# A tail with three more tiles turned on TensorE, and an even plan for the DMAs of the backward attention loop

## The chip, the cores and the metric

The kernel runs on one core of one Trainium2 chip. The metric is device time in microseconds (us) of one execution. Lower is better. The core has a matmul engine (PE in the profile, its weight loads PEld), VectorE (DVE), ScalarE (ACT), GpSimd (POOL) and SyncE (SP), and queues of DMAs that SP, ACT and POOL issue.

## The reference

One transformer block, forward and backward: layer norm with a modulation from a conditioning vector, attention with 32 heads of width 16 over 2048 tokens of width 512, a second modulated norm, and a two-layer net with a squared ReLU. The output of the block and the gradients of nine inputs are wanted.

```python
def _fwd_reference(A_x, A_wqkv, A_wo, B_x, B_w1, B_b1, B_w2, B_b2, c, w_mod):
    ...
    mod = (_silu(c) @ w_mod).reshape(c.shape[0], 6, 1, -1)
    sa, ca, ga, sb, cb, gb = (mod[:, 0].copy(), mod[:, 1].copy(), mod[:, 2].copy(), mod[:, 3].copy(), mod[:, 4].copy(), mod[:, 5].copy())
    h = _layernorm(x, axis=-1) * (1 + ca) + sa
    x = x + ga * _A_ref(h, A_wqkv, A_wo)
    h = _layernorm(x, axis=-1) * (1 + cb) + sb
    x = x + gb * _B_ref(h, B_w1, B_b1, B_w2, B_b2)
    return x
...
    _out, _vjp = jax.vjp(_f, A_x, A_wqkv, A_wo, B_w1, B_b1, B_w2, B_b2, c, w_mod)
    _grads = _vjp(grad_out)
    _out0 = jnp.asarray(_out)
    return (_out0, *[jnp.asarray(_g) for _g in _grads])
```

`_A_ref` is the attention (`x @ wqkv`, softmax of the scaled scores, `@ wo`), `_B_ref` the net. All arrays are bf16.

## The kernel before

The forward pass, the net and its gradients fill the first 1120 us and are not touched. The change lies in the two stages behind them.

**The loop** is the backward pass of the attention. It runs over 8 groups of 4 heads (called heads here, `hg`), and in each over 4 chunks of 512 keys (`kc`) and 16 tiles of 128 queries, so 512 units. For each unit PE makes the scores of four heads (`score`), ACT their exponentials `E_u` (`expo`), PE the products with the gradient `dO` (`dp_pair`, two per unit, each of two heads), DVE multiplies these with `E_u` into `dS_u` (L1600), and PE sums the gradients of keys and values in `accVK` (`k_quad`, `v_quad`) and of queries in `dqacc` (`dq_quad`), the last from a transposed `dS`. Most of `dS` is transposed by DMA from SP (L1615, L1617), one unit of eight on PE (`pe_turn`). Four units make a block.

The order of the work on each engine is written by hand: the strings `order_t` and `order_n` list the steps of a block, and `manual_schedule` keeps each engine to that order. The step `D` counts the pairs of products (`nD`, 128 to a head, 1024 in all). After each `D` all the DMAs that `at(j, ...)` has put down for a pair up to that count are issued. `load` issues them from ACT, in line with its exponentials. They are

- per head 22 loads for the next head (`kvq_loads`, `row_loads`: q, k, v, dO rows and two auxiliary rows), planned by `plan_head`, and the step `spread_qz` on POOL,
- the stores of a head's dV/dK columns, one per `kc` (L1657), and of its dQ, four rows of 16 (L1689), in DRAM tensors `dVKtP` and `dQc`,
- in heads 4 to 6, 24 loads of `wT_st`, the transposed `wqkv`, into columns 0 to 255 of `KS_tok` and `dOs_tok`, which the heads 0 to 3 have left,
- in the last head 40 loads of 16 rows that bring back four groups of dV/dK (`xs["vk", 0]` to `xs["vk", 3]`) and one tile of dQ (`xs["dq", 0]`).

**The tail** begins before the last units are done. Its inputs are eight tiles of dV/dK and four of dQ (`xs`), each 128 rows of features by 2048 tokens. It does two things with them. `dh1(t, srcs)` (L1778) multiplies 128 tokens of each tile with the turned weights, twelve matmuls per token tile `t`, seven of them early (`early7`) and five late (`late`), whose tiles arrive last; `ln_grad`, `norm_tile` and `dx_out` carry the result through the layer norm on DVE and ACT. `dwqkv` (L1970) multiplies the normed input `h1J` with the tiles in token order: 12 blocks of 16 matmuls, four on `tokA` (dV/dK 0 to 3), four on `tokB` (dV/dK 4 to 7), four on `KS_tok` (dQ). For that each tile is transposed: `turn_vk` does it on PE with copies on DVE (tiles 0 to 3, into `tokA`), `turn_dma` by a DMA from SP (tiles 4 to 7 and all four of dQ). dQ goes into `KS_tok`, whose columns 0 to 255 hold turned weights until the last `dh1`.

Beside this the tail makes the gradient of the modulation: `mod_row(k)` (L1872) is one matmul that picks a row out of `rowsb` (a copy by POOL of the sums, two rows of it scaled by DVE in `factors`) into a bank `px`, and an ACT copy to `dmodb`; `row_sums(g)` sums four token tiles each into the banks `accVK` and `px`; `wmod_grad` and `c_grad` use the rows, the latter with `w_mod`, which `load_wmod` brings in from SP once the space of `xs["vk", 0]` to `xs["vk", 3]` is free.

Loop and tail are two `manual_schedule` parts (L1714 and L1994).

Of the kernel before, what the change touches and what calls it, by code (L numbers as in the profile page):

```python
# [34 lines left out]
def kernel(  # L35
# [1499 lines left out]
    with ExitStack() as ph:  # L1535
# [134 lines left out]
        def dq_out(b):  # L1670
# [30 lines left out]
        for hg in range(1, HG):  # L1701
            plan_head(hg)
        pieces = []
        for i, key in enumerate(("q", "k", "v", "do")):
            xs["vk", i] = hsets[0][key][:]
        xs["dq", 0] = qz[0].rearrange("p t h d -> p (t h d)")
        for (key, i), dsrc in zip([("vk", 0), ("vk", 1), ("vk", 2), ("vk", 3), ("dq", 0)], (dVKtP,) * 4 + (dQc,)):
            pieces += [(xs[key, i][r:r + 16, :], dsrc[i][r:r + 16, :]) for r in range(0, P, 16)]
        for i, (to, fro) in enumerate(pieces):
            at((HG - 1) * 128 + 14 + 27 * i // 10, load, to, fro)  # L1710
        for i in range(24):
            j, r = i // 2, slice(64 * (i % 2), 64 * (i % 2) + 64)
            at((4 + i // 8) * 128 + 106 + 4 * (i % 8), load, w_rows(j)[r], wT_st[j].rearrange("p (a b) -> p a b", a=2)[r])
        with tc.manual_schedule(engines={PE.engine, ACT.engine, DVE.engine, SP.engine, POOL.engine}):  # L1714
# [68 lines left out]
            def turn_vk(i):  # L1783
                for g in range(2):
# [4 lines left out]
                    for i8 in range(8):  # L1789
                        t = 8 * g + i8  # L1790
                        PE.transpose(pt[:, i8, :], xs["vk", i][:, t * P:(t + 1) * P], identb[:])
                    DVE.tensor_copy(tokA[:, i, 8 * g:8 * g + 8, :], pt[:])
# [28 lines left out]
            turn_vk(0)  # L1821
# [12 lines left out]
    with ExitStack() as ph:  # L1834
# [3 lines left out]
        rowsb = big.tile([P, D], BF, name="rowsb")  # L1838
# [16 lines left out]
        def constants():  # L1855
            POOL.memset(thirty2[:], 1.0 / 32)
            POOL.tensor_copy(selb[:], identb.rearrange("p (j c) -> p j c", c=32)[:, :, 0:1].to_broadcast([P, 4, P]))
            POOL.tensor_copy(rowsb[0:97, :], sums[0:97, :])
# [4 lines left out]
        def factors():  # L1863
            DVE.tensor_scalar(nrd[:], rstd1[:], -1.0 / D, None, ALU.mult)
            DVE.reciprocal(rec4, cb1_bc)
            for r in (32, 64):
                DVE.tensor_tensor(rowsb[r:r + 1, :], sums[r:r + 1, :], rec4[r:r + 1, :], ALU.mult)

        def mod_row(k):
            j = (5, 3, 4, 2)[k]  # L1870
            pm = psx.tile([P, 512], F32, name="pmod", tag="px")
            PE.matmul(pm[:], selb[0:97, k, :], rowsb[0:97, :], start=True, stop=True)  # L1872
# [90 lines left out]
        def dwqkv(n, b, ic):  # L1963
# [7 lines left out]
            wblk = big.tile([P, D], BF, name="wqblk", tag="wqblk", bufs=3)  # L1971
# [12 lines left out]
        def turn_dma(key, i):  # L1984
            if key == "vk":
                if not tokB:
                    tokB["t"] = tpool.tile([P, 4, TT, P], BF, name="dvk_tokB", tag="dsT")
# [6 lines left out]
        with tc.manual_schedule(engines={PE.engine, ACT.engine, DVE.engine, SP.engine, POOL.engine}):  # L1994
# [11 lines left out]
            for t in range(2):  # L2006
                dh1(t, early7[6:])
            for t in range(2, 6):
                dh1(t, early7)
            load_x0(3)  # L2010
            for t in range(TT):
# [4 lines left out]
                if 1 <= t < 5:  # L2016
                    mod_row(t - 1)
# [6 lines left out]
                if t in (6, 8, 10, 12):  # L2024
# [95 lines left out]
```

## Time and profile before

| | us |
|---|---|
| median of 3 runs | 2492.26 |
| lowest, highest | 2484.49, 2504.86 |
| the profiled execution | 2491.55 |
| its span | 2489.4 |
| the loop, first to last product on DVE (1120.1 to 2372.9) | 1252.8 |
| from there to the end | 116.5 |

Over the span PE is busy 93%, ACT 92%, DVE 73%, POOL 15%. The busy time of PE does not mean that it runs at its peak, since matmuls overlap: a 512-column matmul is recorded with some 380 ns and the next starts some 216 ns after it. So the tail is read by the times at which groups of matmuls begin and end, and by who ended PE's waits. In a table of stretches the columns are the length, the busy time and the number of instructions of each engine, the granted share of the TensorE clock, the share of the DMA engines and the GB/s. The chain of waits is read from its end back: each line is a start, a length, and the work or DMA that the next line waited for.

### The profile page before, as it was taken

The page shows a single profiled execution, that of the slowest core. Times are in us where ns is not written, and L with a number is a line of the kernel's source. Part 1 is how long each engine was busy: PE and PEld are TensorE (multiplying, and loading weights), DVE is VectorE, ACT ScalarE, POOL GpSimd, SP SyncE. Part 2 cuts the span into 40 slices and gives each one's busy share as a digit, 9 for nine tenths or more (in the row PEclk, how much of TensorE's full clock was granted, in tenths as well). Part 3 has the DMA queues.
Part 4 walks back from the last instruction along what each step waited for, and adds up shares of the span by engine and source line. Part 5 has one row for each costly group of instructions (what it writes and reads, how often), then busy time and mean ns, then how long its engine had stood idle before and what let it go on. Part 6 is the DMA issues. An engine that isn't in the chain of part 4 may idle for free.

```text
span 2489.4 us, 49493 instructions
## 1 busy us (share of the span) xinstructions
PE 2313.2 (93%) x18745; PEld 767.8 (31%) x18826; DVE 1809.5 (73%) x2354; ACT 2301.3 (92%) x3582; POOL 372.5 (15%) x412
## 2 busy tenths in 40 slices
PE   8898889989988998999999999999999999999988
PEld 3232223222322332442323223333332223332233
DVE  5555153454435454578999999999999999998974
ACT  7999999999989999639999999999999999999953
POOL 2000000211323142201111101111011110110112
PEclk9999999999999999999999999999999999999999
DMA  4466555366757765979999999999999999999997
GB/s 141 134 170 170 152 123 131 97 163 144 104 85 172 152 120 131 253 228 171 206 201 198 204 202 200 209 206 206 207 207 210 198 207 203 205 205 204 194 221 174
DMA packets 1222523, 442.38 MB, mean 178 GB/s; under 512 B 1099246, under 2 KB 1195116, under 8 KB 1222028
## 3 DMA queue, kind: packets, MB, share of 16 engines
q1 hardware_dynamic: 1186028, 393.47, 82.6%
q0 software_dynamic: 14544, 23.47, 5.9%
q10 hardware_dynamic: 21712, 22.27, 3.7%
q8 instruction: 148, 2.42, 0.4%
q14 instruction: 91, 0.75, 0.1%
HBM read 94.63 MB, written 70.78 MB: 66 GB/s over the span
## 4 chain that ended last, share of the span: by engine, by line
ACT 42%; PE 38%; issue 8%; DVE 6%; DMA 3%; SPq 1%; ACTq 1%; POOL 0%; another core or an unknown queue 0%; DVEq 0%; POOLq 0%
ACT E_u L1584 24%; ACT ET L566 13%; PE dqacc L1667 4%; PE psST L564 4%; PE psS_A L1578 3%; PE pm L232 3%; ACT dsT L1754 2%; PE accVK L1640 2%; PE psS_B L1578 2%; PE oacc L580 2%; PE pm L413 2%; PE pm L399 2%; PE psS_C L1578 2%; PE accVK L1649 2%; PE pm L488 1%
## 5 line engine op out<-in xcount | busy, mean ns | idle before, releaser
L1600 DVE TENSOR_TENSOR dS_u<-psD_u,E_u 128x1024 bf16<-128x1024 f32 x1024 | 1186.9, 1218 | 69.0 <-PE psD_u L1598 27.8
L566 ACT ACTIVATE ET<-psST 128x1024 bf16<-128x1024 f32 x1024 | 941.3, 1257 | 19.5 <-PE psST L564 19.1
L1584 ACT ACTIVATE E_u<-psS_A 128x512 bf16<-128x512 f32 x768 | 508.4, 662 | 12.3 <-PE psS_C L1578 8.5
L1584 ACT ACTIVATE E_u<-psS_B 128x512 bf16<-128x512 f32 x768 | 502.2, 654 | 7.1 <-PE psD_u L1598 2.1
L1598 PE MATMUL psD_u<-iv,ido 32*128 32x512 bf16 x2048 | 408.9, 388 | 0.0
L564 PE MATMUL psST<-qt_sb,kt_sb 32*128 32x512 bf16 x2048 | 317.3, 385 | 61.2 <-ACT ET L566 46.5
L1584 ACT ACTIVATE E_u<-psS_C 128x512 bf16<-128x512 f32 x512 | 333.2, 651 | 4.0 <-PE accVK L1649 1.7
L1578 PE MATMUL psS_A<-ik,iq 32*128 32x512 bf16 x768 | 293.5, 382 | 12.8 <-ACT E_u L1584 2.7
L1578 PE MATMUL psS_B<-ik,iq 32*128 32x512 bf16 x768 | 295.3, 384 | 9.3 <-ACT E_u L1584 1.6
L1578 PEld LDWEIGHTS <-iq 32*128 32x128 bf16 x2048 | 130.1, 91 | 318.1 <-issue 300.7
L1640 PE MATMUL accVK<-dS_u,qz 128*32 128x512 bf16 x2048 | 212.0, 390 | 0.2 <-PE psD_u L1598 0.2
L580 PE MATMUL oacc<-ET,vaug 128*32 128x512 bf16 x2048 | 207.1, 394 | 3.0 <-DVE ostage L584 3.0
L1685 POOL TENSOR_TENSOR dQacc<-dQacc,dqtmp 128x512 f32<-128x512 f32 x64 | 81.2, 1268 | 853.4 <-ACT dqtmp L1680 729.2
L1649 PE MATMUL accVK<-E_u,dOs_tok 128*16 128x512 bf16 x2048 | 203.5, 387 | 0.0
L1578 PE MATMUL psS_C<-ik,iq 32*128 32x512 bf16 x512 | 194.6, 380 | 5.4 <-ACT E_u L1584 1.2
L564 PEld LDWEIGHTS <-kt_sb 32*128 32x128 bf16 x2048 | 85.7, 91 | 349.0 <-issue 324.5
L1667 PE MATMUL dqacc<-dsT,KS_tok 128*32 128x512 bf16 x2048 | 147.3, 386 | 14.3 <-ACT E_u L1584 0.7
L1754 ACT ACTIVATE dsT<-ptT 128x1024 bf16<-128x1024 bf16 x126 | 143.5, 1139 | 5.6 <-PE ptT L1630 5.0
L250 DVE COPY part<-pm 128x512 f32<-128x512 f32 (+2 forms) x103 | 63.5, 617 | 112.4 <-PE pm L232 105.6
L1598 PEld LDWEIGHTS <-ido 32*128 32x128 bf16 x2048 | 104.4, 91 | 96.3 <-issue 90.8
L1640 PEld LDWEIGHTS <-qz 128*32 128x32 bf16 x2048 | 58.1, 94 | 180.5 <-issue 166.0
L584 DVE COPY ostage<-oacc 128x512 f32<-128x512 f32 x32 | 22.1, 689 | 101.0 <-PE oacc L580 87.1
(417 smaller groups left out, 2524.2 us busy)
## 6 DMA issues: line engine op xcount, KB each, us to landing
p_st<-part POOLq DMA_DIRECT2D x36, 256.0 KB, 5.1
kt_sb<-qkT_st SPq DMA_DIRECT2D x124, 64.0 KB
wA<-in_B_w_dram SPq DMA_DIRECT2D x28, 256.0 KB
wB<-w1T_st SPq DMA_DIRECT2D x21, 256.0 KB
wA<-w2T_st SPq DMA_DIRECT2D x21, 256.0 KB
wB<-in_B_w_dram SPq DMA_DIRECT2D x21, 256.0 KB
p_st<-part POOLq DMA_DIRECT2D x25, 192.0 KB, 4.9
p_st<-part SPq DMA_DIRECT2D x18, 256.0 KB
```

The source lines that it names most:

```text
L564: PE.matmul(ps[:, hi, :], kt_sb[r:r + 32, kt * P:(kt + 1) * P], qt_sb[r:r + 32, :], start=True, stop=True, tile_position=(r, 0))
L566: ACT.activation(ET[:, 2 * pair:2 * pair + 2, :], ps[:], AF.Exp, scale=SCALE)
L580: PE.matmul(oacc[32 * hq:32 * hq + 32, :], lhsT, ET[:, hq, :], start=(kt == 0), stop=(kt == TT - 1), tile_position=(0, 32 * hq), skip_grou ...
L1578: PE.matmul(psS[:], st["q"][r:r + 32, qt * P:(qt + 1) * P], st["k"][r:r + 32, kc * 512:kc * 512 + 512], start=True, stop=True, tile_positi ...
L1584: ACT.activation(bst[u][0][:, hq, :], sst.pop((u, hq))[:], AF.Exp, scale=SCALE)
L1598: PE.matmul(psD[:, hi, :], st["do"][r:r + 32, qt * P:(qt + 1) * P], st["v"][r:r + 32, kc * 512:kc * 512 + 512], start=True, stop=True, til ...
L1600: DVE.tensor_tensor(dS_u[:, 2 * pair:2 * pair + 2, :], psD[:], E_u[:, 2 * pair:2 * pair + 2, :], ALU.mult)
L1640: PE.matmul(cur["vk"][32 * hq:32 * hq + 32, :], hst[hg]["qz"][:, qt, hq, :], bst[u][1][:, hq, :], start=(qt == 0), stop=False, tile_positi ...
L1649: PE.matmul(acc[32 * hq:32 * hq + DH, :], dOs_tok[:, qt, (hg * 4 + hq) * DH:(hg * 4 + hq + 1) * DH], E_u[:, hq, :], start=False, stop=(qt ...
L1667: PE.matmul(acc[32 * hq:32 * hq + 32, :], KS_tok[:, kc * 4 + kt, h * DH:h * DH + 32], tT[:, :, hq * 4 + kt, :], start=(kt == 0), stop=(kt ...
L1685: POOL.tensor_tensor(dst2, dst, tmp[:], ALU.add)
L1754: ACT.activation(dst, pt[:], AF.Identity)
```

## The change

The loop's DMAs get one plan per head. `plan_head(h)` now lists all loads of a head (for the last head the 40 pieces; in heads 4 to 6 eight `wT_st` loads each are put between) and the stores that will come up in it, and gives each a place: the k-th of `count` at pair 10 + 111 k / count of the head. A store takes a place once its earliest pair has come; a load takes one from pair 14 on. What is left over goes behind pair 124. The stores keep to their place or to the moment when their data is there, whichever is later. The `wT_st` loads are cut by columns (128 rows of 256) and not by rows (64 rows of 2 x 256).

In the tail, dV/dK tiles 6 and 7 and the dQ tile 3 are turned on PE, the last with ACT copies. The other three dQ transposes alternate with the loads of `w_mod`. Two rows of the modulation (0 and 3) are picked before the loop over token tiles, from a second copy of the sums, the other two at tiles 4 and 5; two x loads go behind the last dQ rows on SP; the row sums come one tile later, the third behind the first block of `dwqkv`. Loop and tail become one schedule. `wqblk` shares the buffers of `xn1b`.

```diff
-        def plan_head(hg):
-            j0 = (hg - 1) * 128 + 14
-            loads = list(kvq_loads(hg)) + list(row_loads(hsets[hg % 2]["do"], dOT_st, hg, slice(0, n), d_st))
-            for i, (to, fro) in enumerate(loads):
-                at(j0 + (4 * i if i < 4 else 36 + 36 * (i - 4) // 10), load, to, fro)
-            at(j0 + 40, spread_qz, hg)
+        store_at = {}
+
+        def plan_head(h):
+            loads = []
+            if h + 1 < HG:
+                loads += list(kvq_loads(h + 1)) + list(row_loads(hsets[(h + 1) % 2]["do"], dOT_st, h + 1, slice(0, n), d_st))
+            else:
...
+            if 4 <= h < 7:
+                for i in range(8 * (h - 4), 8 * (h - 4) + 8):
+                    j, a = divmod(i, 2)
+                    loads.insert(6 + 3 * (i % 8), (w_rows(j)[:, a, :], wT_st[j][:, 256 * a:256 * a + 256]))
+            stores = [(26 + i, ("dq", h - 1, i)) for i in range(4) if h > 0]
+            stores += [(32 * kc + 41, ("vk", h, kc)) for kc in range(3) if h < HG - 2]
+            stores += [(9, ("vk", h - 1, 3)) for _ in range(1) if 0 < h < HG - 1]
+            stores.sort()
+            count = len(loads) + len(stores)
+            for k in range(count):
+                j = 10 + 111 * k // count
+                if stores and (stores[0][0] <= j or not loads):
+                    store_at[stores.pop(0)[1]] = h * 128 + j
+                elif j >= 14:
+                    at(h * 128 + j, load, *loads.pop(0))
+            for k, (to, fro) in enumerate(loads):
+                at(h * 128 + 124 + k, load, to, fro)
...
+            if h + 1 < HG:
+                at(h * 128 + 54, spread_qz, h + 1)
...
-                    at(cur["j"] + 4, load, dVKtP[hg][:, part], hst[hg]["vk"][:, part])
+                    at(max(cur["j"] + 4, store_at["vk", hg, kc]), load, dVKtP[hg][:, part], hst[hg]["vk"][:, part])
...
-                    at(hg * 128 + 158 + 4 * hq, load, dQc[hg // 2, r:r + DH, :], st["dq"][32 * hq:32 * hq + DH, :])
+                    at(max(cur["j"] + 6, store_at["dq", hg, hq]), load, dQc[hg // 2, r:r + DH, :], st["dq"][32 * hq:32 * hq + DH, :])
...
-        for i, (to, fro) in enumerate(pieces):
-            at((HG - 1) * 128 + 14 + 27 * i // 10, load, to, fro)
-        for i in range(24):
-            j, r = i // 2, slice(64 * (i % 2), 64 * (i % 2) + 64)
-            at((4 + i // 8) * 128 + 106 + 4 * (i % 8), load, w_rows(j)[r], wT_st[j].rearrange("p (a b) -> p a b", a=2)[r])
...
+        hold.enter_context(tc.manual_schedule(engines={PE.engine, ACT.engine, DVE.engine, SP.engine, POOL.engine}))
...
-        with tc.manual_schedule(engines={PE.engine, ACT.engine, DVE.engine, SP.engine, POOL.engine}):
-            for g in range(3):
+        if True:
+            for g in range(2):
                 load_x0(g)
             nb1_rows()
-            turn_vk(1)
+            turn_vk(("vk", 1), tokA[:, 1])
             last_dq(B_last, slice(3 * 512, n))
             constants()
-            turn_vk(2)
-            turn_vk(3)
+            load_x0(2)
+            load_x0(3)
+            turn_vk(("vk", 2), tokA[:, 2])
+            turn_vk(("vk", 3), tokA[:, 3])
+            tokB["t"] = tpool.tile([P, 4, TT, P], BF, name="dvk_tokB", tag="dsT")
+            for t in range(2):
+                dh1(t, early7[6:])
+            mod_row(0, "px")
+            turn_vk(("vk", 6), tokB["t"][:, 2])
+            dh1(2, early7)
+            mod_row(3, "accVK")
+            turn_vk(("vk", 7), tokB["t"][:, 3])
             factors()
             norm_tile(0)
             norm_tile(1)
-            for t in range(2):
-                dh1(t, early7[6:])
-            for t in range(2, 6):
+            for t in range(3, 6):
                 dh1(t, early7)
-            load_x0(3)
             for t in range(TT):
...
-                if 1 <= t < 5:
-                    mod_row(t - 1)
+                if 4 <= t < 6:
+                    mod_row(t - 3, ("accVK", "px")[t - 4])
...
-                if t in (6, 8, 10, 12):
+                if t in (6, 8):
                     turn_dma("vk", 1 + t // 2)
...
-                if t % 4 == 3 and t > 4:
-                    row_sums(t // 4 - 1)
+                if t % 4 == 0 and t > 4:
+                    row_sums(t // 4 - 2)
             for i in range(4):
+                if i < 3:
+                    turn_dma("dq", i)
                 load_wmod(i)
-            for i in range(4):
-                turn_dma("dq", i)
...
                 if k == 0:
+                    row_sums(2)
                     dx_out(TT - 1)
...
+                if k == 4:
+                    turn_vk(("dq", 3), KS_tok[:, :, 3 * P:4 * P], ACT)
```

More of the change, by code (lines that the diff above doesn't have):

```diff
@@ L1790, in turn_vk @@
                         t = 8 * g + i8
-                        PE.transpose(pt[:, i8, :], xs["vk", i][:, t * P:(t + 1) * P], identb[:])
-                    DVE.tensor_copy(tokA[:, i, 8 * g:8 * g + 8, :], pt[:])
+                        PE.transpose(pt[:, i8, :], xs[i][:, t * P:(t + 1) * P], identb[:])
+                    if eng is DVE:
+                        DVE.tensor_copy(dst[:, 8 * g:8 * g + 8, :], pt[:])
+                    else:
+                        ACT.activation(dst[:, 8 * g:8 * g + 8, :], pt[:], AF.Identity)
             def copy_turn(half):
@@ L1837 @@
         rec1, rec4 = (hsets[i]["qs"].rearrange("p t e -> p (t e)").bitcast(F32) for i in range(2))
-        rowsb = big.tile([P, D], BF, name="rowsb")
+        rowsb = [big.tile([P, D], BF, name=f"rowsb{i}") for i in range(2)]
         selb = big.tile([P, 4, P], BF, name="selb")
@@ L1857, in constants @@
             POOL.tensor_copy(selb[:], identb.rearrange("p (j c) -> p j c", c=32)[:, :, 0:1].to_broadcast([P, 4, P]))
-            POOL.tensor_copy(rowsb[0:97, :], sums[0:97, :])
+            for i in range(2):
+                POOL.tensor_copy(rowsb[i][0:97, :], sums[0:97, :])
         def nb1_rows():
@@ L1866, in factors, with mod_row @@
             for r in (32, 64):
-                DVE.tensor_tensor(rowsb[r:r + 1, :], sums[r:r + 1, :], rec4[r:r + 1, :], ALU.mult)
-        def mod_row(k):
+                DVE.tensor_tensor(rowsb[1][r:r + 1, :], sums[r:r + 1, :], rec4[r:r + 1, :], ALU.mult)
+        def mod_row(k, tag):
             j = (5, 3, 4, 2)[k]
-            pm = psx.tile([P, 512], F32, name="pmod", tag="px")
-            PE.matmul(pm[:], selb[0:97, k, :], rowsb[0:97, :], start=True, stop=True)
+            pm = psx.tile([P, 512], F32, name="pmod", tag=tag)
+            PE.matmul(pm[:], selb[0:97, k, :], rowsb[int(k % 3 != 0)][0:97, :], start=True, stop=True)
             ACT.activation(dmodb[:, j, :], pm[:], AF.Identity)
@@ L1993 @@
         early7 = early + (("vk", 7),)
-        with tc.manual_schedule(engines={PE.engine, ACT.engine, DVE.engine, SP.engine, POOL.engine}):
-            for g in range(3):
+        if True:
+            for g in range(2):
                 load_x0(g)
             nb1_rows()
-            turn_vk(1)
+            turn_vk(("vk", 1), tokA[:, 1])
             last_dq(B_last, slice(3 * 512, n))
             constants()
-            turn_vk(2)
-            turn_vk(3)
+            load_x0(2)
[10 more added lines that the diff above has]
+            turn_vk(("vk", 7), tokB["t"][:, 3])
             factors()
```

23 lines of the change are left out of this document (11 added, 12 removed).

## The prediction

> **What bounds the kernel now.** I read the page for the span, then the stretches (a table by windows), then the chain of waits through the end, then the waits of each engine. The profiled execution took 2491.55 us by the clock outside, 2489.4 us of it span; 2.15 us lie around it. The median of the runs is 2492.26, so sums against 2491.55 need +0.7.
>
> ```profile
> span 2489.4 us, 49493 instructions
> ```
>
> The stretches, each with its length, then busy time and instructions of PE, PEld, DVE, ACT and POOL, the granted clock, the DMA share and GB/s. First the loop of eight heads (1024 pairs of products on DVE, 128 to a head), then its best head (3) and its last (7), then the tail in six pieces.
>
> ```profile
> core 0: us, PE busy (x) PEld busy (x) DVE busy (x) ACT busy (x) POOL busy (x), PEclk, DMA share, GB/s
> 1120.10:2372.90 1252.80, 1205.43 (x11466) 374.37 (x11466) 1185.64 (x1023) 1224.20 (x2329) 145.53 (x106) 0.98 1.20 202
> 1591.10:1745.30 154.20, 148.72 (x1442) 46.86 (x1440) 148.13 (x129) 153.05 (x293) 17.95 (x13) 1.00 1.20 207
> 2214.20:2372.90 158.70, 151.92 (x1430) 46.12 (x1428) 147.46 (x128) 151.99 (x288) 15.22 (x12) 0.96 1.22 201
> 2372.90:2384.40 11.50, 11.01 (x152) 7.24 (x151) 6.23 (x10) 3.78 (x5) 2.19 (x2) 1.00 1.12 229
> 2384.40:2395.30 10.90, 7.74 (x39) 3.33 (x37) 6.26 (x7) 1.60 (x3) 1.61 (x4) 1.00 0.83 221
> 2395.30:2405.80 10.50, 7.50 (x25) 2.78 (x26) 9.22 (x26) 7.78 (x12) 1.29 (x1) 0.84 0.85 287
> 2405.80:2434.80 29.00, 29.00 (x151) 12.38 (x150) 24.57 (x65) 20.77 (x29) 6.98 (x7) 1.00 1.02 171
> 2434.80:2464.90 30.10, 30.10 (x144) 13.16 (x140) 22.92 (x61) 14.31 (x31) 9.91 (x14) 1.00 1.12 257
> 2464.90:2489.40 24.50, 16.37 (x64) 6.90 (x65) 0.00 (x0) 5.58 (x11) 3.48 (x6) 0.82 0.26 81
> ```
>
> The loop has PE, DVE and ACT all at 95% or more: a head without disturbance costs 154.2 us, eight of them 1233.6, so the loop loses 19.2 us to single stalls. The tail is TensorE's: two pieces are full, and what is lost stands in three, where PE is idle or its clock is below 1. Who ends those waits, on PE in the tail:
>
> ```profile
> PE pwx L1970 <- DMA KS_tok<-iq: 3.9, 1, 3.9
> PE pmod L1872 <- ACT dmodb L1873: 3.0, 3, 1.3
> PE pdh L1778 <- DMA iq<-dQst: 2.3, 1, 2.3
> PE pdh L1778 <- DMA qz<-dVKtP: 0.8, 1, 0.8
> ```
>
> So 10.0 us of waits (total, times, longest), each touched by the change. The chain through the end shows what the clock adds:
>
> ```profile
> 2412.26 0.55 PE rsumJ L1942 x8
> 2412.80 10.47 PE pdh L1778 x48
> ...
> 2434.83 7.01 PE pwq L1970 x32
> ...
> 2468.82 0.59 PE pwx L1970
> 2469.41 0.22 issue
> 2469.63 5.34 PE pwx L1970 x14
> ```
>
> A 512-column matmul costs 10.47/48 = 0.218 us in step, a block of dwqkv (16) 7.01/2 = 3.5 us; the block behind the wait for KS_tok took 0.59 + 0.22 + 5.34 = 6.15, 2.65 too long, at the clock of 0.82.
>
> **The change, part by part.** Signs: minus is time won.
>
> *Three more tiles on PE.* The price of a turned tile, by the nearest rows (the same helper, same shapes), with the work of DVE and POOL that stands around the place where two of them go:
>
> ```profile
> 2383.54 1.06 PE L1791 MATMUL ptv<-identb,ido 128*128 128x128 bf16 x16
> ```
> ```profile
> 2383.90 1.88 DVE L1792 COPY dvk_tokA<-ptv 128x1024 bf16<-128x1024 bf16 x3
> 2385.69 0.35 DVE L1864 TENSOR_SCALAR rstd<-rstd 128x16 f32<-128x16 f32 x1
> 2385.95 3.34 DVE L1865 RECIPROCAL iqs<-modbc 128x512 f32<-128x512 bf16 x1
> 2389.39 1.38 DVE L1867 TENSOR_TENSOR rowsb<-r_inv,iqs 1x512 bf16<-1x512 f32 x2
> ```
> ```profile
> 2385.40 0.61 POOL L1858 CAST rowsb<-r_inv 97x512 bf16<-97x512 f32 x1
> ```
>
> About 1.0 us of PE each. Tiles 6 and 7 fall into 2384.4 to 2395.3, where PE has 10.90 - 7.74 = 3.16 us idle, waiting for dV/dK and dQ rows. Two mod rows come along (0.44 us). Row 0 waits for POOL's copy of the sums, ready at 2385.40 + 0.61 = 2386.0; PE stands there two matmuls after 2384.4, at 2384.9, so a wait of 1.1 us, with all of dh1 queued behind it. Stretch: 7.74 + 2.0 + 0.44 + 1.1 = 11.3 against 10.9, **+0.4**. The rows that PE waited for (2.3 and 0.8 us) are met 0.4 us after they used to land, and SP now issues the dQ rows ahead of two x loads that stood before them, so they should cost nothing. DVE gains four copies (1.88/3 = 0.63 each, 2.5 us) ahead of the 5.1 us of factors; its first dxn comes at about 2396, as before.
>
> *Mod rows out of the first tiles.* In 2395.3 to 2405.8 the pmod matmuls wait 3.0 us for ACT's copies out of the one bank; 25 matmuls at 0.218 need 5.45 us, were busy 7.50, at a clock of 0.84, after the waits before it. If neither is left: -3.0 - 2.05, and two rows (0.44) gone: **-5.5**. Late next is DVE: in the full stretch its six instructions a tile cost 24.57/65 x 6 = 2.27 us, PE's twelve matmuls 2.62, so PE stays the slower. The two rows that stay at tiles 4 and 5 hold both banks that the first row sums need; their wait for ACT costs about one of the three pmod waits, **+1.0** (0 to 1.3). The third row sums only move (0.55 us) behind dwqkv 0.
>
> *dQ: three transposes between the w_mod loads, one on PE.* The rows of SP's issues now:
>
> ```profile
> 2437.40 12.45 SPq L1991 DMA_TRANSPOSE KS_tok<-qz  x1
> 2449.89 5.26 SPq L1991 DMA_TRANSPOSE KS_tok<-ik  x1
> 2455.19 4.80 SPq L1991 DMA_TRANSPOSE KS_tok<-ido  x1
> ```
>
> The first stood behind eight loads. It now comes first, as soon as dh1's last matmul frees the columns of KS_tok that held the turned weights. Row sums stood behind that matmul, so it ended at 2434.83 - 0.55 = 2434.3; with the terms so far, 4.1 less, it is 2430.2. Three transposes take 5 us each; the eight loads cost the first 12.45 - 5 = 7.5, so the four that now lie ahead of the last cost 3.7; 5 us to land (the flight of 4.98 below): 2430.2 + 15 + 3.7 + 5 = 2454. The first block that reads them starts eight blocks later, 2430.2 + 8 x 3.5 = 2458 even without the row sums, totals and turned tile between. So no wait: **-3.9 - 2.65**, and **+1.0** for the tile turned on PE; its two ACT copies lie in a stretch where ACT is busy 14.31 of 30.10 us.
>
> *One schedule.* The order on PE, DVE, ACT and SP within the loop is unchanged but for ACT's DMA issues; DVE's small factor for the mean moves from the program's start to here (about the 0.35 of L1864, DVE idle): 0.
>
> *The even plan in the loop.* Places: one DMA per 3.7 pairs in heads 1 to 3 (30 of them in 111 pairs), 2.9 in heads 4 to 6, 2.5 in head 7. Before, 18 loads lay in 61 pairs (one per 3.4) with stores added, and in head 7 one per 2.7 with four dQ stores thrown among them. There the trace has a stall:
>
> ```profile
> 2251.57 8.46 DMA dsT<-dS_u
> 2260.03 0.02 issue
> 2260.05 0.33 ACTq L1560
> ```
>
> ACT's issue of a load waited until SP's transpose of 8.46 us had landed; the exps queued behind it on ACT, PE ran short and its clock fell (0.96 in that head). Head 7 lost 158.7 - 154.2 = 4.5 us. Spaced, I expect most of this back. The other heads' losses show no DMA that I can name, so I give them nothing: **-3** (-19.2 if all vanish, +6 if a like stall comes up in a head that has none). By the Trainium skill (DMA: Bandwidth & Descriptors, Issuing engines are not separate DMA queues) DMAs of all issuers run on the same 16 engines, so spreading wins no bandwidth; the trace's DMA share of 1.20 to 1.22 in good and bad heads agrees. By it this term would be 0.
>
> *End of the loop.* The plan leaves two of head 7's pieces over, put behind the 124th pair; in ACT's order the last has five exps behind it. Row of the first of those five, of the matmuls that need the piece, and of a load's flight there:
>
> ```profile
> 2369.88 0.60 ACT L1584 ACTIVATE E_u<-psS_B 128x512 bf16<-128x512 f32 x1
> ```
> ```profile
> 2372.66 1.40 PE pdh L1778 x6
> ...
> 2380.66 4.98 DMA iv<-dVKtP
> ```
>
> 2369.9 + 4.98 = 2374.9; the sixth matmul stands at 2373.9: **+1.0** (0, or 4.4 with the flight of 8.46).
>
> Sum: 0.4 - 5.5 + 1.0 - 6.55 + 1.0 - 3 + 1.0 = **-11.7**; 2491.55 - 11.7 = 2479.9, say **2480 us**.
>
> **The rivals.** *The dQ transposes are late all the same* (2488 to 2494): at 12.45 us each, as the one behind eight loads, they land at 2430 + 37 + 5 = 2472, a wait of some 11 us, and the clock falls again (2.65): 2480 + 14 = 2494; at half of that wait 2488. For it: POOL's output DMAs run at the same time. Against: the two later ones took 5.26 and 4.80 beside the same outputs. 0.14.
>
> *A late last row at every head* (2514, slower): the plan leaves one load of each head, the delta row of the next, for pair 124, four pairs (4 x 154.2/128 = 4.8 us) ahead of the matmul that reads it. The flights in the rows are 4.98 to 8.46. If it comes late, seven times a stall like the one in head 7: 7 x 4.5 = 31.5, less the tail's 8.7. It decides once the flight passes the lead. Against: ACT's exps run ahead of DVE's products, which lengthens the lead by a pair or two. 0.08.
>
> *The loop loses its stalls altogether* (2464): -19.2 in place of -3. For: an even load of the DMA queues. Against: the clock dips in heads without any late DMA. 0.12.
>
> *The clock halves under the turned tiles* (2491): 11.3 us of work in that stretch at half clock in the worst case. Against: the stretch 2372.9 to 2384.4, most of its 152 PE instructions transposes, was granted 1.00. 0.05. The Trainium skill (TensorE: Matmul & The Clock Gate, PE-mode transpose) says that transposes do not count as busy for the clock and cost about 275 ns each in a kernel; 48 of them would be 13 us, not 3, an estimate that makes 2490. The trace's 16 in 1.06 us speaks against that.
>
> **How the numbers follow.** The forecast has 0.61. About 1% (25 us) is what this kernel's measurement tells from no change. Own range of the forecast: terms of unknown size (loop -8 to +3, end of loop to +4.4, row sums) and the scatter of the runs: 2469 to 2492. The late transposes lie in it or at 2494; 2464 and 2497 leave out half of the loop's best case, most of the slow one and a little else. Faster than 2467.3 needs the loop's gain: 0.11. Slower than 2517 needs the late row at its worst: 0.04. Within 1%: 0.85.
>
> **What would show it.** In the tail: no PE wait for KS_tok and the blocks of dwqkv even at 3.5; pmod waits of at most 1.3 us together; dh1's last matmul near 2430 (less what the loop wins); one new wait on POOL's sums. In the loop: head 7 near 155, no ACT issue waiting for a transpose. Wrong would be: the chain through a DMA of KS_tok again, PE waiting for ido at each head's first products, or clock dips in more heads than before.

## The result, and the profile after

| | before | after |
|---|---|---|
| median | 2492.26 us (11 runs, 2478.7 to 2504.86) | 2476.98 us (11 runs, 2471.62 to 2486.92) |
| ratio to before, 95% interval | | 0.9946, 0.9923 to 0.9969 |
| profiled execution, span | 2491.55, 2489.4 us | 2478.99, 2477.2 us |
| the loop, first to last product on DVE | 1252.8 us | 1250.3 us |
| from there to the end | 116.5 us | 105.4 us |

The forecast was 2480 us, the range 2464 to 2497. The interval leaves out 1: the kernel is faster by 0.5%, within the 1% of "no change". Of the 12.2 us between the two spans, 11.1 lie in the tail.

The stretches of the changed kernel, with the columns of before: the loop, its last head, then the tail from the last product on.

```profile
span 2477.2 us, 49668 instructions
```
```profile
core 0: us, PE busy (x) PEld busy (x) DVE busy (x) ACT busy (x) POOL busy (x), PEclk, DMA share, GB/s
1121.50:2371.80 1250.30, 1206.98 (x11466) 375.77 (x11466) 1183.82 (x1024) 1224.15 (x2329) 145.85 (x106) 0.98 1.20 203
2217.10:2371.80 154.70, 149.42 (x1428) 46.70 (x1428) 146.85 (x129) 151.29 (x288) 15.23 (x12) 0.99 1.24 204
2371.80:2384.00 12.20, 11.01 (x153) 7.28 (x151) 6.31 (x11) 3.78 (x5) 2.23 (x2) 1.00 1.12 241
2384.00:2396.00 12.00, 10.96 (x77) 5.86 (x75) 9.29 (x13) 3.42 (x5) 2.11 (x5) 1.00 0.84 216
2396.00:2408.50 12.50, 12.50 (x59) 5.55 (x57) 11.94 (x34) 9.18 (x12) 2.50 (x2) 1.00 1.04 265
2408.50:2428.50 20.00, 19.89 (x103) 8.59 (x102) 19.37 (x54) 17.00 (x25) 5.36 (x5) 1.00 0.83 151
2428.50:2450.00 21.50, 21.50 (x119) 9.77 (x118) 11.59 (x21) 11.67 (x24) 7.32 (x10) 1.00 1.08 222
2450.00:2474.00 24.00, 23.91 (x112) 10.67 (x109) 12.28 (x42) 10.05 (x20) 6.51 (x11) 1.00 0.60 191
```

Before, three of the tail's stretches had PE idle by 3 to 8 us, two of them with a clock of 0.82 to 0.84. Now the clock is 1.00 in all, and PE waits more than 0.25 us in two places only. These are the waits of PE over the tail (total, times, longest):

```profile
PE pmod L1893 <- POOL rowsb L1879: 1.0, 1, 1.0
PE dqacc L1694 <- DMA dsT<-dS_u: 1.0, 1, 1.0
```

The second still belongs to the loop (its last dQ products). The chain of waits through the end shows how solid the rest is. Its columns are start, length, work:

```profile
2390.46 3.25 DVE iqs L1886
...
2395.22 0.69 DVE dxn L1936
...
2408.53 0.59 ACT dmodb L1894
...
2409.56 10.47 PE pdh L1795 x48
2420.03 0.55 PE rsumJ L1963 x8
2420.57 7.88 PE pdh L1795 x36
2428.45 3.45 PE pwq L1991 x16
...
2448.73 0.89 PE ptv L1808 x16
...
2459.99 3.45 PE pwx L1991 x16
2463.44 6.91 PE pwq L1991 x32
2470.35 3.47 PE pwx L1991 x16
```

The chain of before ran through a DMA of `KS_tok` and 5.34 us of slow matmuls. Now it passes through DVE's `factors` and norm gradients up to 2408, and from there through matmuls alone. The blocks of `dwqkv` are even at 3.45 to 3.56, and the four that read `KS_tok` begin at 2459.99 without a wait; the last transpose into it had landed at 2456.0.

### The profile page after: what moved, and what is told of

The parts are those of the page before. It is cut to its first block, busy times and chain, and to the rows that moved or that the text cites. A ratio compares the mean times of both kernels' runs of the same rounds, so it can differ in the third digit from the quotient of the medians.

```text
span 2477.2 us, 49668 instructions
## 1 busy us (share of the span) xinstructions
PE 2321.9 (94%) x18874; PEld 770.8 (31%) x18874; DVE 1809.2 (73%) x2358; ACT 2303.7 (93%) x3584; POOL 372.6 (15%) x413
## 5 line engine op out<-in xcount | busy, mean ns | idle before, releaser
L1605 PE MATMUL psS_A<-ik,iq 32*128 32x512 bf16 x768 | 293.2, 382 | 11.2 <-DVE dwlast L236 0.9
```

Source lines behind the costliest of these rows:

```text
L1605: PE.matmul(psS[:], st["q"][r:r + 32, qt * P:(qt + 1) * P], st["k"][r:r + 32, kc * 512:kc * 512 + 512], start=True, stop=True, tile_positi ...
```

## The experiments

All edits are against the changed kernel unless they say otherwise (minus: its line; plus: the experiment's). "Tail" is the time from the last product on DVE to the end, "loop" from the first to the last product, both from the trace. A "spell" is a stretch in which the trace shows TensorE's granted clock at half. Where one run is named, a difference in its whole time of some us tells nothing, and its trace is read instead.

**Each kernel once more.**

> The changed kernel once more, for a second trace. If the halvings of the TensorE clock in the loop are chance (a matter of phase), they fall in other heads than in the first trace (where they cost heads 1, 0 and 5 most) while their number stays 6 to 12 and the tail agrees within 0.5 us; if the DMA plan makes them, they come back in the same heads and at the same pairs. Time 2472 to 2485.

> The kernel before once more, for a second trace of it. Theory A, its tail is a fixed 116 to 117 us with a wait of 3 to 5 us for the last dQ tile: then the tail's gain of 11 us belongs whole to the changed tail. Rival B, that wait comes and goes with what still moves on the DMA engines when dh1 ends, as in the kernel with the old tail and the new plan, whose tail took 110.2 with no such wait: tail 109 to 113. The clock's dips in the loop lie at other places than in the first trace under both, and the loop takes 1246 to 1258 us.

The changed kernel: median 2478.62 (12 runs) beside 2490.58 (29 runs), ratio 0.9945, 0.9922 to 0.9967. Its second trace has a tail of 105.3 and a loop of 1246.5, with the spells of low clock at other places in the loop than in the first. The kernel before, in one run: 2487.03, loop 1256.4, tail 110.6, not 116.5. PE waits in that trace, over the tail:

```profile
PE pmod L1872 <- ACT dmodb L1873: 3.5, 2, 2.6
PE pwx L1970 <- issue: 2.2, 1, 2.2
PE pdh L1778 <- DMA iq<-dQst: 1.6, 1, 1.6
```

The `pwx` wait ended 0.1 us after the last transpose of dQ had landed (2466.8), so it is the wait for `KS_tok` again, 2.2 us instead of 3.9, without a low clock behind it. The 116 to 117 us of theory A did not come back; the tail is in rival B's range. The changed tail repeats within 0.1 us; the tail of before does not, and its gain is 5 to 11 us by the trace one takes.

**Tail alone, loop alone.** The first kernel is the changed one with the DMA places of before (`plan_head`, the pieces, the `wT_st` loads and the stores), the second the kernel before with the changed places. The first's edit, cut to the stores:

```diff
-                    at(max(cur["j"] + 4, store_at["vk", hg, kc]), load, dVKtP[hg][:, part], hst[hg]["vk"][:, part])
+                    at(cur["j"] + 4, load, dVKtP[hg][:, part], hst[hg]["vk"][:, part])
...
-                    at(max(cur["j"] + 6, store_at["dq", hg, hq]), load, dQc[hg // 2, r:r + DH, :], st["dq"][32 * hq:32 * hq + DH, :])
+                    at(hg * 128 + 158 + 4 * hq, load, dQc[hg // 2, r:r + DH, :], st["dq"][32 * hq:32 * hq + DH, :])
```

> The changed tail with the old DMA plan of the loop. 'Tail' is the time from the start of the last product on DVE to the end of the span (116.5 us before, 105.5 in the changed kernel). Theory A (the tail earns nearly all, the plan about 3 us): tail 105 to 107, loop 1250 to 1257 with a stall in head 7 again (158 us), time about 2480, ratio 0.995 to 0.996. Rival B (the even plan earns it, or the tail gains only because the loop leaves its DMA queues empty): tail 110 or more, time 2487 or more.

> The new DMA plan of the loop with the old tail. Theory A: tail 116 to 118 with PE's waits for KS_tok (3 to 5 us), for the pmod bank (3) and for the dQ rows (3) all back; loop 1247 to 1254, head 7 near 155; time 2487 to 2492, ratio 0.998 to 1.000. Rival B: ratio 0.996 or less.

Both beside 2490.58 (29 runs): tail alone 2482.02 (12 runs), ratio 0.9958, 0.9936 to 0.9980; loop alone 2484.49 (12 runs), ratio 0.9969, 0.9944 to 0.9994. In the traces, tail alone: tail 105.4, loop 1250.6; loop alone: tail 110.2, loop 1257.5. So the changed tail takes its 105.4 under either plan, as theory A had it. The plan alone made the kernel faster too, with a ratio between those of its two theories, but its profiled loop was the longest of the plan's; it also had the most time at half clock of them, 58.0 us against 30.7 to 44.4. Its tail kept the waits for the mod rows and for the dQ row (2.6 and 3.6 us), and had none for `KS_tok`.

**The order on SP, the dQ tile, the two dV/dK tiles.** Three kernels take the "three more tiles" and "dQ" steps apart. The first has the `w_mod` loads ahead, as before, and then the three transposes:

```diff
             for i in range(4):
-                if i < 3:
-                    turn_dma("dq", i)
                 load_wmod(i)
+            for i in range(3):
+                turn_dma("dq", i)
```
The second has dQ tile 3 turned by DMA again, alternating like the others:

```diff
-                if i < 3:
-                    turn_dma("dq", i)
+                turn_dma("dq", i)
...
-                if k == 4:
-                    turn_vk(("dq", 3), KS_tok[:, :, 3 * P:4 * P], ACT)
```
The third has dV/dK tiles 6 and 7 turned by DMA again:

```diff
-            turn_vk(("vk", 6), tokB["t"][:, 2])
...
-            turn_vk(("vk", 7), tokB["t"][:, 3])
...
-                if t in (6, 8):
+                if t in (6, 8, 10, 12):
                     turn_dma("vk", 1 + t // 2)
```

> Only the order on SP is undone: all eight w_mod loads first, then the three dQ transposes (the fourth tile stays on PE). My step: the first transpose takes 12 us to issue, the three land some 12.5 + 5 + 5 + 5 = 27 us after dh1's last matmul plus 5 us for the loads, 32 us in all; the blocks that read them start 32 to 33 us after it (8 blocks, two row sums, totals, the turned tile): a wait of 0 to 2 us, so tail 105.5 to 108. Rival (the order is what earns the whole 6.5 us): a wait of 4 us and a halved clock, tail 111 to 112.

> Only the turning of dQ tile 3 on PE is undone: four dQ transposes, each ahead of a w_mod load. My step priced the turned tile at +1.0 us and four transposes at 5 us with 0.9 us per load: landed at 2430.2 + 20 + 5.6 + 5 = 2461 against a need at 2461.5 (last tile, same clock as the prediction): tail 104.5 to 107. Rival (it is needed): the wait is 3 us or more and the clock falls, tail 109 or more.

> Only dV/dK tiles 6 and 7 go back to DMA transposes at token tiles 10 and 12. My step gave the two tiles +2.0 us of PE work in a stretch where PE waited 3.2 us for rows. Theory A (the work was hidden in that wait): tail 105 to 106.5 from that side; behind it, the two transposes stand in front of the dQ ones on SP, but end before dh1 does, so no more than 1 us. Rival A2 (the gap returns and halves the clock): tail 107 to 110. Rival A3 (turning them cost PE 2 us): tail 103.5.

| | time (one run) | tail | PE's wait for `KS_tok` | dQ transposes by DMA: first issue to last landing |
|---|---|---|---|---|
| changed kernel | 2478.99 | 105.4 | none | 3: 2428.5 to 2456.0, 27.5 us |
| w_mod loads first | 2476.69 | 106.4 | none | 3, behind 8 loads: 2424.2 (first load) to 2454.3, 30.1 us |
| dQ tile 3 by DMA | 2490.47 | 116.6 | 8.5 | 4: 2428.8 to 2467.7, 38.9 us |
| tiles 6, 7 by DMA | 2478.28 | 111.8 | 5.5 | 3: 2425.0 to 2456.7, 31.8 us |

The order on SP is worth nothing that shows, within what was expected: the 1.0 us more of that tail is a wait of 1.8 us at the loop's end (`pdh` for `qz<-dQc`, the leftover piece) in place of the 1.0 for `dsT` there. One transpose more costs all that the tail had won. PE at the wait for it, by time (start, length, what, and in brackets the idle time ahead and its releaser):

```profile
2467.90 0.59 PE L1991 MATMUL pwx<-KS_tok,h1J 128*128 128x512 bf16 x1 [8.53 <-DMA KS_tok<-iq]
2468.70 5.74 PE L1991 MATMUL pwx<-KS_tok,h1J 128*128 128x512 bf16 x14 [0.22 <-issue]
```

Its 11.2 us more are the wait of 8.5 and 3.1 for the block behind it at a lower clock (0.59 + 0.22 + 5.74 against 3.47), less 0.9 for the tile that PE no longer turns: 10.7. I had thought tile 3 would fit; the price of a transpose by DMA was too low. And the two dV/dK tiles, whose transposes SP issues at 2412 and 2418, ahead of dh1's end, cost 6.4 us, which none of the three theories gave. 5.5 of it is a wait, and not where they were taken out but at the first block of dQ:

```profile
2456.82 0.59 PE L1991 MATMUL pwx<-KS_tok,h1J 128*128 128x512 bf16 x1 [5.47 <-issue]
```

The row names "issue", but the last transpose had landed at 2456.73, 0.09 us earlier. SP's own rows in that kernel tell how it got late:

```profile
L2010 SPq DMA_TRANSPOSE dvk_tokB<-vkb x2: 5403/6282/7162, 2412.3 to 2417.7; - x2
L2010 SPq DMA_TRANSPOSE dvk_tokB<-iv x1: 8008/8008/8008, 2394.6 to 2394.6; - x1
L2010 SPq DMA_TRANSPOSE dvk_tokB<-qz x1: 8960/8960/8960, 2403.2 to 2403.2; - x1
L2010 SPq DMA_TRANSPOSE KS_tok<-qz x1: 11319/11319/11319, 2425.0 to 2425.0; - x1
```

(Least, median and most ns of one, then the first and last start.) The first dQ transpose took 11.3 us of SP with no load between it and the transposes ahead of it; in the changed kernel the same one took 2.9. So it is not the eight loads alone that make a transpose slow. The queue has a part here too: dh1's last matmul ended at 2419.8, but SP was at the fourth dV/dK transpose until 2424.9, so the first dQ transpose started 5.1 us late, where in the changed kernel it starts at once. With the 4.3 us that the three then took longer (31.8 against 27.5), less the 4.0 us that they were early there, that makes 5.4, the wait. Why the transposes ahead of it took 8.0 and 9.0 us, where the changed kernel's took 5.7 and 3.6, is not shown.

**Is it SP's queue, or are the DMA engines full?** The kernel with dQ tile 3 by DMA, which here leaves out most writes of the gradient of `w_mod`, so that output is not complete:

```diff
-            if k == len(js) - 1:
+            if k == len(js) - 1 and ic == 0:
                 POOL.dma_start(out=out_9[ic * P:(ic + 1) * P, js[0] * D:(js[-1] + 1) * D].rearrange("p (j d) -> p j d", d=D),
```

> Against the kernel with all four dQ tiles turned by DMA, which waited 8.5 us for the last one: six of the eight writes of w_mod's gradient are left out (those of rows 128 and up: 2.25 MB that POOL would write while the tiles are turned), nothing else. In that kernel's trace the DMA engines are busy all through from 2428 to 2468. Theory A, the DMA engines are full and the transposes' time is set by what moves beside them: without the writes (at 200 to 250 GB/s, 9 to 11 us of the engines) the four transposes end some 6 to 10 us earlier, the wait for the last falls to 0 to 3 us, and the tail is 105 to 110 instead of 116.6. Rival B, the order and the issue of the transposes on SP's queue set it (about 10 us each, whatever else moves): the wait stays at 7 to 9 us and the tail at 115 to 117.

It took 2477.65 (one run), tail 106.5, and no wait for `KS_tok` is left. The four transposes, in the same order on the same queue, ran from 2426.8 to 2450.7, 23.9 us instead of 38.9. Theory A holds: the same queue and order give no wait once POOL writes less, so what the four transposes lacked was time of the DMA engines. The DMA engines in the kernel with the wait, from 2428 to 2468 (busy tenths in 40 slices, then the queue that SP uses and the one that POOL uses):

```profile
DMA  7192999869999999999699998999999999999999
...
q1 hardware_dynamic: 9273, 4.81, 65.4%
q0 software_dynamic: 1688, 3.93, 45.5%
```

The same view with the writes left out, from 2426 to 2451:

```profile
q1 hardware_dynamic: 9278, 4.84, 78.1%
q0 software_dynamic: 845, 1.14, 30.4%
```

POOL's packets took 45.5% of 40 us, 18.2, and now 30.4% of 25, 7.6: 10.6 us less. SP's packets are as many in both (9273 and 9278), but took 65.4% of 40, 26.2, and now 78.1% of 25, 19.5: each is quicker too when POOL writes less. The two together are 17.2 us, more than the 15.0 by which the transposes got shorter; the shares of one stretch add up to over 100%, so packets overlap, and the sum can't be exact.

**The mod rows.** First all four back to tiles 1 to 4 and one bank ("rows late"):

```diff
-            mod_row(0, "px")
...
-            mod_row(3, "accVK")
...
-                if 4 <= t < 6:
-                    mod_row(t - 3, ("accVK", "px")[t - 4])
+                if 1 <= t < 5:
+                    mod_row(t - 1, "px")
```
And, the other way, row 0 behind the tile turned next ("row 0 later"):

```diff
-            mod_row(0, "px")
             turn_vk(("vk", 6), tokB["t"][:, 2])
+            mod_row(0, "px")
```

> Only the mod rows go back to token tiles 1 to 4 and to one bank. My step: -5.5 us came from PE's three waits for ACT (3.0) and the clock they halve. Theory A: three pmod waits of 2.5 to 3.5 us together, tail 108 to 111 with a halved clock, 108 without one. Rival (DVE is the bound of those tiles anyway, since the chain now runs through ln_grad from 2390 to 2408): tail 105.5 to 106.5 although the waits are back.

> In the tail, the first row of mod's gradient is computed after the tile turned next instead of ahead of it, so that PE has about 1 us of other work (16 transposes, 1.06 us in step) where it waited 1.04 us for POOL's row sums. Theory A: the wait goes, or falls under 0.3 us, and since PE then runs without a break to the end, the tail is 0.8 to 1.0 us shorter: 104.3 to 104.6 against 105.3 to 105.4. Rival B: DVE's factors and its chain of norm gradients, which the chain of waits passes through between 2390 and 2408, set the end of that part: the wait goes, a wait of the same length comes back at dh1's row sums or norm gradients, and the tail stays at 105.2 to 105.5. The time of the whole, 2471 to 2487, tells nothing of 1 us.

Rows late: 2483.18 (one run), tail 109.8, 4.4 more, as theory A had it. Two `pmod` waits for ACT's copies are back (4.1 us, for the 1.0 on POOL), and a spell of 3.4 us behind them. Row 0 later: 2472.74 (one run), tail 104.0. In place of the 1.0 us wait on POOL stands

```profile
PE pmod L1893 <- POOL rowsb L1879: 0.2, 1, 0.2
```

and nothing came up behind it (of the 1.4 us, 0.5 are a shorter wait for `dsT` at the loop's end). So that wait was real time although the chain of waits runs through DVE beside it.

**The late last row.** The rival of the prediction that ended slower hung on the lead of one load per head.

```diff
-                at(h * 128 + 124 + k, load, to, fro)
+                at(h * 128 + (127 if h + 1 < HG else 124 + k), load, to, fro)
```

> The one load that the new plan leaves over at the end of each head (the delta row of the next head) goes out at pair 127 instead of 124, for the seven heads that have a next one; the last head's five are not moved. In the changed kernel's trace this load is issued 7.2 us ahead of the next head's first product and lands 2.2 to 4.8 us ahead of it. Theory A, the lead at pair 124 was short but enough and its end is real: three pairs later (3 x 1.2 = 3.6 us) it lands from 1.4 us late to 1.2 us early, and the matmul that reads it must run about a product ahead, so PE waits for the row 1 to 3.5 us at most heads: loop 7 to 20 us longer (1255 to 1270), time 2485 to 2498. Rival B, ACT issues its DMA far ahead of DVE whatever the pair, so the load has slack: loop 1246 to 1252 as before, no PE wait for ido, time 2472 to 2487.

It took 2510.14 us (one run beside one of the changed kernel, 2478.52), loop 1282.7: 32 us more than the changed kernel's for a load put 3 pairs (3.6 us) later, beyond what theory A gave. PE's waits ahead of its products, and the loop's stretch:

```profile
PE psD_u L1625 <- DMA ido<-d_st: 10.5, 4, 3.6
PE psD_u L1625 <- DVE dS_u L1627: 4.3, 4, 1.5
```
```profile
1119.80:2402.50 1282.70, 1226.01 (x11466) 377.62 (x11466) 1184.80 (x1023) 1228.14 (x2329) 145.68 (x106) 0.96 1.16 197
```

Seven of these eight waits, 14.5 us, stand at the 128th pair of the seven heads, ahead of the next head's first products; in three of them the last to release PE was a product on DVE, and the row need not have been late there. 14.5 us of waits do not make 32. The rest goes with the clock: in the trace each of these seven places has a spell of its own (half clock for 3.4 to 13.7 us), and all spells of the loop add up to 99.0 us, against 44.4 in the changed kernel. One of the heads, before and behind its wait:

```profile
1598.00:1600.50 2.50, 2.50 (x22) 0.68 (x18) 2.50 (x3) 2.50 (x6) 0.32 (x1) 1.00 1.49 150
1600.50:1603.00 2.50, 0.32 (x2) 0.00 (x0) 1.55 (x2) 1.37 (x3) 0.00 (x0) 0.93 0.91 118
1603.00:1610.00 7.00, 5.56 (x35) 2.09 (x35) 2.45 (x2) 2.95 (x5) 0.00 (x0) 0.54 0.88 179
```

PE stands for 3.6 us (0.32 busy in the middle row), and the clock of the next 7 us is 0.54. So the 54.6 us more at half clock cost 32.4 - 14.5 = 17.9, an estimate of 0.33 us for each; in the changed kernel the loop's 1250.3 - 1233.6 = 16.7 us above eight undisturbed heads go with 44.4 us at half clock, 0.38 for each.

**Both findings put in.** Row 0 later, and the last row of each head at pair 122:

```diff
-                at(h * 128 + 124 + k, load, to, fro)
+                at(h * 128 + (122 if h + 1 < HG else 124 + k), load, to, fro)
...
-            mod_row(0, "px")
             turn_vk(("vk", 6), tokB["t"][:, 2])
+            mod_row(0, "px")
```

> The changed kernel with two of the runs' findings put in: the first row of mod's gradient after the tile turned next (in one trace that took the 1.04 us wait on POOL's row sums away, tail 104.0), and the delta row of each next head at pair 122 instead of 124, 2.4 us earlier, since at 124 its lead is so short that four of the traces show one PE wait of 0.6 to 1.0 us for it and at 127 the loop grew by 32 us. Theory A, both were real: tail 104.0 to 104.5, no PE wait for ido in the loop, loop 1246 to 1251; the time 1 to 2 us under the changed kernel's 2477 to 2479, ratio to the kernel before 0.993 to 0.995, which the interval cannot tell from the changed kernel's 0.9946. Rival B, the earlier row lies closer to the even plan's last transfers and delays a transpose of the last tiles of the head: PE waits of 0.5 to 2 us for dsT in the loop, loop 1251 to 1257, ratio 0.996 or more.

Median 2475.80 (12 runs) beside 2490.26 (17 runs), ratio 0.9941, 0.9921 to 0.9961. Tail 104.5, loop 1250.1, no PE wait for `ido`; but PE waits for transposed dS, 0.9 of it behind the last product and 3.0 in the loop, where the first trace of the changed kernel had none:

```profile
PE dqacc L1694 <- DMA dsT<-dS_u: 3.9, 3, 1.8
```

The tail is 0.9 shorter, as A had it. In the loop PE waits for transposes as B had it, without a longer loop; but with the row at pair 124 this wait was 0 to 2.9 us from trace to trace, so one trace does not show that the earlier row makes it. Against the kernel before it is a gain; against the changed one (0.9946, 0.9945) the intervals lie on each other, and whether it is better stays open.

## Why the prediction was right, point by point

**The time** came out 3 us below the forecast. The sum of the tail's terms was -8.7 (with +1.0 for the loop's end); against the trace it was made from, the tail gave -11.1, against the second trace of the same kernel -5.2. The medians differ by 15.3 in the first comparison and 12.0 in the second, so the whole sum (-11.7) was about right, but not every term was. Nor do the tail's steps add up: undone one at a time, dQ tile 3, the two dV/dK tiles and the mod rows cost 11.2, 6.4 and 4.4 us, 22 together, more than the whole tail won. They share one wait. With four dQ transposes the last lands 95.6 us behind the loop's last product, before it was 95.8 (92.4 in the second trace), so whatever ends dh1 earlier would only have made the wait for `KS_tok` longer. That the terms came out near the measured sum all the same is in part luck.

- *Three more tiles, +0.4.* Their cost on PE was as priced: 0.89 to 1.06 us a tile, clock 1.00 throughout, with the wait on POOL that was foreseen (1.04, 1.1 given) and the two waits for dV/dK and dQ rows gone. What failed is that their benefit stood at nothing. The step counted PE, DVE and SP's order, and no time of the DMA engines. The two dV/dK tiles alone are worth 6.4 us (111.8 against 105.4), 5.5 of it a wait some 70 us behind the place for which the step was worked out, to which SP's order added, by starting the first dQ transpose 5.1 us late.
- *Mod rows, -5.5 and +1.0.* Sum -4.5; undone, 4.4. Here wait, clock and rows were each counted, and it held. DVE as the next engine was foreseen too: its first `dxn` was given for 2396 and starts at 2395.2. The +1.0 itself did not show: PE has no such wait in the trace.
- *dQ, -6.55 and +1.0.* The last transpose was given to land at 2454 with the need at 2458; it landed at 2456.0 with the need at 2460.0. The slack of 4 is right by luck (in the second trace it was 6.9), and the reason is wrong: I took 5 us for each transpose and 3.7 for the loads ahead. They took 2.9, 6.9 and 8.7 us on SP, and the alternation that the sum relied on is worth nothing (106.4, none of it at `KS_tok`). What clears the wait is one transpose less on full DMA engines: with four, the third landed at 2461.9 and the fourth at 2467.7, 11.7 us later than the last of three. Also, 3.9 was one draw; the second trace of before had 2.2, and the old tail behind the new plan none.
- *The even plan, -3.* The loops with the changed plan and no experiment in it took 1246.5 to 1257.5 in nine traces, mean 1250.2, the three with the old places 1250.6 to 1256.4, mean 1253.3. The difference is the -3, but the two ranges overlap, because the time at half clock differs from trace to trace. At the same 44.4 us of it the old places took 1252.9 and 1256.4, the changed ones 1250.1 to 1250.9 (three traces); at 30.7 us, 1250.6 and 1246.5. So like for like the plan wins 2 to 6 us. What it takes away are PE's waits for ACT's exponentials, here before (three lines) and in the changed kernel (one), from 1122 to 2360:

```profile
PE psS_A L1578 <- ACT E_u L1584: 2.4, 6, 1.1
PE psS_B L1578 <- ACT E_u L1584: 1.2, 4, 0.5
PE psS_C L1578 <- ACT E_u L1584: 1.2, 3, 0.4
PE psS_B L1605 <- ACT E_u L1611: 0.6, 2, 0.5
```

  They come to 4.5 to 5.0 us in the three traces with the old places and to 0.2 to 1.6 in the nine with the changed ones. That is the mechanism of the prediction, exponentials held up on ACT, but only a third of it stands in head 7; the rest lies in heads that the step gave nothing, in all three traces near pair 117 of heads 4 to 6 and near pair 103 of one to four heads. That the kernel gets faster by the plan is shown by the ratio of the loop alone (0.9969, interval up to 0.9994), which does not tell loop from tail. The stall that I named is gone in the changed kernel: head 7 took 154.7, and no ACT issue there waits for a transpose. But heads 0 and 1 took 161.3 and 158.0 in that trace against 159.5 and 154.9, so naming one stall of one trace got the size by chance: ACT was idle for 1.0 us at the 8.46 us transpose, and the rest of that head's 4.5 goes with 13.7 us at half clock in it, and the spells come at other places in each trace.
- *End of the loop, +1.0 (0 to 4.4).* 0 in the first trace, 1.6 and 1.8 in two others (`pdh` for `qz<-dQc`). Within its bounds.
- *One schedule, 0.* Not tried alone.

**The rivals.** "The dQ transposes are late" came true once one more tile was left to DMA: 2490.47, where the rival said 2488 to 2494. "A late last row" is real, and nearer than its 0.08 felt: at pair 124 four traces show one PE wait of 0.6 to 1.0 us for that row, and three pairs on the time was 2510, where the rival said 2514; the 32.4 us over seven heads are 4.6 each, near the 4.5 that it took from head 7. "The loop loses all stalls" did not come near. "The clock halves under the turned tiles" did not happen. The Trainium skill (TensorE: Matmul & The Clock Gate, PE-mode transpose) gives about 275 ns for one transpose in a kernel, which the prediction multiplied by 48 to an estimate of 13 us. One is recorded here with 219 ns, but 16 take 0.89 to 1.06 us, since they overlap: it was wrong to multiply a length where steps add up. The Trainium skill's rule that DMAs of all issuers run on the same 16 engines (DMA: Bandwidth & Descriptors, Issuing engines are not separate DMA queues) I had held against the loop's plan only; the trace agrees with it in the tail, where SP's four transposes took 23.9 us instead of 38.9 when POOL wrote less.

## What to carry to other kernels

Ask of each transfer what it takes of the 16 DMA engines, not only when its queue issues it: where their busy row reads mostly 9, moving transfers within the queue gave nothing, taking one away gave 11 us and two others 6, and the wait that those two caused stood some 70 us later, at another tensor. Do not add up steps that shorten the way to one and the same wait. Read the size of a wait from more than one trace before it is credited to a change; here one and the same wait was 3.9 and 2.2 us. Compare loops at the same time at half clock. And where a load is planned a few us ahead of its use in a loop that is full, price the step past its lead: 3.6 us of delay, seven times, cost 32.

## What the runs showed of the hardware

- A transpose by DMA of 128 x 2048 bf16 (512 KB) took SP 2.2 to 12.9 us to issue in these tails, by what else moved and stood ahead of it; four in a row with eight loads between took 38.9 us beside 3.9 MB of POOL's writes and 23.9 beside 1.1 MB. The 9,273 packets of SP's queue in that stretch moved 4.81 MB: of the 10,962 packets of all queues there, 8,674 are under 512 bytes.
- TensorE's clock fell to half in spells of 3.4 us or a multiple of it (6.8, 10.2, 13.7). Where PE had stood for the late row, one began within the wait or up to 1.4 us behind it, in every head. Most others come with no PE idle time over 0.2 us in the 16 us before them, some 20.5 us apart: at 1320.9, 1341.4 and 1361.9 in the changed kernel. Their places are no chance: each of the changed kernel's ten spells behind the loop's first 3 us begins within 0.1 us of a transpose of the unit that is turned on PE (`pe_turn`, tile `ptT`), and so do 92 of the 121 in all fourteen traces, where some 6% of the time lies that close. One of them, the transposes and the stretch with its clock of 0.50:

```profile
1341.40 1.01 PE L1657 MATMUL ptT<-identb,dS_u 128*128 128x128 bf16 x8
1341.40:1344.80 3.40, 3.40 (x19) 1.08 (x19) 2.95 (x3) 3.04 (x5) 0.00 (x0) 0.50 1.22 217
```

  What ties the two stays open: no run moved or left out that unit, most of its turns bring no spell, and the tiles turned in the tail brought none. Which turns have one differs from trace to trace of one kernel.
- The part before the loop, the same in all these kernels, ended between 1114.2 and 1124.2 us. That scatter of 10 us is nearly as large as the change's effect, and is why stretches, not times of single runs, were compared.
